# A spectral mixer with a token MLP, forward and backward: x's normal form made again on GpSimd, gradient blocks placed by hand, a mean column moved to TensorE

## The chip, the core and the metric

The kernel runs on one NeuronCore of a Trainium2 chip. A core has five instruction streams that run beside each other and meet only at semaphores: TensorE (PE; its weight loads are listed apart, as PEld), VectorE (DVE), ScalarE (ACT), GpSimd (POOL) and SyncE (SP). SP computes nothing; it issues DMAs, and so does GpSimd here. TensorE multiplies a stationary block of at most 128 x 128 (the weights, "lhsT") by a moving block and adds up in PSUM; ScalarE and VectorE copy results from PSUM to SBUF, the working memory of 128 partitions. GpSimd works on SBUF alone in this kernel.

The metric is the device time of one execution in microseconds, lower is better.

## What is computed

The function has two residual blocks on x of 2048 x 448 (S x D, bfloat16), and the kernel returns its output and its gradients for a given grad_out with respect to x, w_r, w_i, w1, b1, w2 and b2.

```python
def _A_ref(x, w_r, w_i):                     # spectral mixer
    X = rfft2(x.astype(float32))             # over S and D; 225 columns kept
    y = irfft2(X * (w_r + 1j * w_i), s=(S, D)).astype(bfloat16)
    return y

def _B_ref(x, w1, b1, w2, b2):               # MLP over the tokens, F = 1792
    h = layernorm(x)
    u = gelu(einsum("bsd,sf->bdf", h, w1) + b1)
    y = einsum("bdf,fs->bds", u, w2) + b2
    return y.transpose(0, 2, 1)

h  = x + _A_ref(layernorm(x), w_r, w_i)
h2 = h + _B_ref(layernorm(h), w1, b1, w2, b2)
out, vjp = jax.vjp(f, x, w_r, w_i, w1, b1, w2, b2); grads = vjp(grad_out)
```

## The kernel before

All tables of the Fourier transforms are constants in DRAM; the transforms themselves are matmuls. A sequence of 2048 rows is held as 16 row tiles of 128 partitions (`NT = 16`), F as 14 blocks of 128 (`NFB = 14`).

The stages, in the order of TensorE's work:

1. Forward rows. x is loaded in four groups of four row tiles. `Norm` (line 298) takes the statistics on DVE (`bn_stats`), the square root on ACT, and writes xln = x * rstd + nb, where nb = -mean * rstd, partly on ACT and partly on DVE. `nb` is a small buffer from a ring. `fft_rows` (331) folds a group into even and odd parts (`eo`, two vector operations and a copy), multiplies by `kf` (342) and copies the results to `zt`.
2. `dg` (468 and on): grad_out times w2, 14 blocks of 16 matmuls (472), each with a transposed load of w2 (`w2T`, ring of four). These blocks need nothing of stage 1 and fill TensorE between the matmuls of `fft_cols` (346), `ifft_cols` (405) and the forward inverse rows, `ifft_rows` (438).
3. `cmul` (389) is the complex product with the filter, on DVE, over six groups of columns (`R_GROUPS`).
4. `gelu_in`, `gelu_out`, `gelu_back` (554 to 586): hidden layer, its activation g and du, the gradient ahead of it. `gb1`, the sum of du over the tokens, is a by-product; line 606 copies it into column D of `du`, so that the matmuls of stage 6 sum it too, as a mean of a row of dh.
5. Output of the forward pass with w2 (`w2c`, 627).
6. dh (666 to 684): for each of 16 row tiles 14 matmuls of w1 transposed with du (449 columns), then `norm_back` (643), the gradient of the layer norm, with the row's mean from column D. Groups of four finished row tiles are folded and transformed by `fft_rows` as they come.
7. The backward mixer: `fft_cols`, `cmul` with w_b, `ifft_cols` give ab2. Then 16 backward rows, `ifft_rows` and `norm_back` with the normal form of x (`xr`) and rstd_x, give the gradient of x.
8. Weight gradients: 14 blocks `gw2(j)` and 16 blocks `gw1(h)`. A block multiplies transposed copies (`g_t` and `goT`, or `hlnT` and `du_t`) in `outer` (200): twelve matmuls over three full slices of D (206) and four over the last 64 columns (213), which go to the two halves of the array. For that the last 64 columns lie twice, in partitions 0 to 63 and 64 to 127 (`ld_twice`). ACT, or DVE for one quarter in some blocks, copies the four PSUM banks to an `s6` or `s4` buffer (ring `w4`, four buffers), and GpSimd issues the store. `grad_w` (749) is another `cmul`, which gives the gradients of w_r and w_i.

Orders. The program is written once, and a scheduler orders the instructions of each engine; where the source gives no order, it takes ready work by its priority. Before, the source has all 16 backward rows, then all gw2 blocks from 1 on, then the gw1 blocks, and the scheduler mixes gradient matmuls in between the rows. `issue_after` puts an instruction behind another one in its engine's order. `nxt` chains SP's loads of the first half in the order of the source; SP issues them one after the other, and an issue can wait for a buffer. The forward's normal form of x is stored to DRAM by four DMAs of this chain (lines 490-491), and read back four row tiles at a time as `xr` by GpSimd's queue (715-717).

`norm_back`, in short: ACT forms v = rstd * ps (+ nm1 in dh's case) in one of three `f2` buffers; DVE forms the row sum nm2 of v times xhat, then xhat * nm2 + v, then adds the residual gradient.

Of the kernel before, what the change touches and what calls it, by code (L numbers as in the profile page):

```python
# [17 lines left out]
P = 128  # L18
S = 2048
D = 448  # L20
# [97 lines left out]
def kernel(  # L118
# [170 lines left out]

    xln_d = dram.tile([P, NT, D], BF16, name="xln_d")  # L290
    xs_d = dram.tile([P, 2, XW], BF16, name="xs_d")
# [6 lines left out]
    class Norm:  # L298
        def __init__(self, src, dst, rstd, eps_col, scale, nm):
            self.src, self.dst, self.rstd, self.eps_col, self.scale, self.nm = src, dst, rstd, eps_col, scale, nm  # L300

        def stats(self, h):
# [9 lines left out]
        def finish(self, g):  # L312
            mv = self.mv[:, :].rearrange("p (i c) -> p i c", c=2)
            r = self.rstd[:, 4 * g:4 * g + 4]
            sq = col(4, f"sq_{self.nm}")
            ac.activation(out=sq[:], in_=mv[:, :, 1], func=ACT.Sqrt, bias=self.eps_col[:], scale=self.scale)
            ve.reciprocal(out=r, in_=sq[:])
            nb = col(4, f"nb_{self.nm}")
            ve.scalar_tensor_tensor(out=nb[:], in0=mv[:, :, 0], scalar=-1.0, in1=r, op0=ALU.mult, op1=ALU.mult)
            for i in range(4):  # L320
                h = 4 * g + i

                if (i > 1 or g == 3) if self.nm == "x" else (i > 1 and g == 3):
                    ve.tensor_scalar(out=self.dst[:, h, :], in0=self.src[:, h, :], scalar1=self.rstd[:, h:h + 1],
                                     scalar2=nb[:, i:i + 1], op0=ALU.mult, op1=ALU.add)
# [62 lines left out]

    def cmul(out, a, b, conj, done=None):
        for r0, r1 in R_GROUPS:  # L390
            n = (r1 - r0) * DF
# [45 lines left out]

    def ifft_rows(ab, itab, h):
        a_t = itab[:, 0:2 * DF].rearrange("p (c k) -> p c k", c=2)
# [4 lines left out]
        for c in range(2):  # L444
            pe.matmul(pq[:, DF:], lhsT=ab[:, 1, c, h, :, :], rhs=b_t[:, c, :], start=(c == 0), stop=(c == 1))  # L445
        eo = k1([P, 2 * DF], "eo2")
        ev(eo[:], pq[:], "a")
        py = ps_sp([P, D])
        pe.matmul(py[:, 0:DF], lhsT=kinv[:, 0, :], rhs=eo[:, 0:DF], start=True, stop=False)  # L449
# [63 lines left out]
    for h in range(NT):  # L513
        py = ifft_rows(ab, di0, h)
        ve.tensor_tensor(out=hn[:, h, :], in0=py[:], in1=x[:, h, :], op=ALU.add)
# [89 lines left out]
    keep(du_d, du, NFB - 2, NFB)  # L605
    ve.tensor_copy(out=du[:, :, D], in_=gb1[:])

# [35 lines left out]
    def norm_back(ps, mean, xhat, rstd_c, back, base, out):  # L643

        v = f2([P, D], "v")
        if mean:
            nm1 = col(1, "nm1")
            ve.tensor_scalar(out=nm1[:], in0=ps[:, D:D + 1], scalar1=rstd_c, scalar2=-1.0 / D,  # L648
                             op0=ALU.mult, op1=ALU.mult)
            ac.activation(out=v[:], in_=ps[:, 0:D], func=ACT.Identity, scale=rstd_c, bias=nm1[:])  # L650
# [62 lines left out]
    ifft_cols(w_b, ab2)  # L713
    for h in range(NT):
        if h % 4 == 0:
# [3 lines left out]
        gx = k1([P, D], "gx")  # L719
        norm_back(py, False, xr[:, h % 4, :], rstd_x[:, h:h + 1], -1.0 / D, dh[:, h, :], gx[:])  # L720
        st(rows(out_1[0])[:, h, :], gx[:])


# [11 lines left out]

    for j in range(1, NFB):
        gw2(j, "aaaa" if j < 8 else "aaav")


# [6 lines left out]
    xs_b = slot(4, [P, 2, XW], "xs_b")  # L746


    def grad_w():
        ld(xs_b[:], xs_d[:])  # L750
        o2 = out_2.rearrange("(q r) k -> q (r k)", r=NR)
        o3 = out_3.rearrange("(q r) k -> q (r k)", r=NR)

        def out(r0, r1):
            return xs_b[:, 0, r0 * DF:r1 * DF], xs_b[:, 1, r0 * DF:r1 * DF]

        def done(r0, r1, last):
            st(o2[:, r0 * DF:r1 * DF], xs_b[:, 0, r0 * DF:r1 * DF])
            st(o3[:, r0 * DF:r1 * DF], xs_b[:, 1, r0 * DF:r1 * DF])

        cmul(out, ds, xs_b, True, done)

# [60 lines left out]
```

## Time and profile before

| what | us |
|---|---|
| median of 3 runs | 367.74 |
| lowest and highest run | 366.51, 368.8 |
| the profiled execution | 367.85 |
| its span, from first to last instruction | 366.1 |
| PE busy in it | 343.1 |
| DVE, ACT, POOL busy in it | 232.3, 210.7, 58.0 |

How the lines are read. In the page, part 1 has busy time, share and count for each engine; part 2 cuts the span into 40 slices and gives the busy share of each as a digit. A timeline row has its start, its duration, the engine ("SPq" is SP's queue: the time that an issue holds it), the line, the operation, output<-inputs, and in brackets how long the engine was idle before it and who ended that. A group of the table of lines has its count after an x, then busy time and mean nanoseconds of one, then the idle time before its members and what ended it. A row of the table of stretches has the stretch, its length, then the busy time and count of PE, PEld, DVE, ACT and POOL, the granted TensorE clock, the busy share of the DMA engines and GB/s. A DMA row has its count, the size of one, and the microseconds from issue to landing. Matmuls overlap, so that one group's busy time runs into the next; distances between starts are safer.

### The profile page before, as it was taken

The page shows a single profiled execution, that of the slowest core. Times are in us where ns is not written, and L with a number is a line of the kernel's source. Part 1 is how long each engine was busy: PE and PEld are TensorE (multiplying, and loading weights), DVE is VectorE, ACT ScalarE, POOL GpSimd, SP SyncE. Part 2 cuts the span into 40 slices and gives each one's busy share as a digit, 9 for nine tenths or more (in the row PEclk, how much of TensorE's full clock was granted, in tenths as well). Part 3 has the DMA queues.
Part 4 walks back from the last instruction along what each step waited for, and adds up shares of the span by engine and source line. Part 5 has one row for each costly group of instructions (what it writes and reads, how often), then busy time and mean ns, then how long its engine had stood idle before and what let it go on. Part 6 is the DMA issues. An engine that isn't in the chain of part 4 may idle for free. (4 is left out here: it accounts for less than half of the span.)

```text
span 366.1 us, 5758 instructions
## 1 busy us (share of the span) xinstructions
PE 343.1 (94%) x2115; PEld 190.9 (52%) x2115; DVE 232.3 (63%) x550; ACT 210.7 (58%) x415; POOL 58.0 (16%) x105
## 2 busy tenths in 40 slices
PE   0899998999999999999999999899999999999994
PEld 0556665676655555555554556355664455544442
DVE  4882779887746999522157778637995555699200
ACT  3474553447649997005612243787767666767573
POOL 1000000001122112400340000100121232337310
PEclk9999999999999999999999999999999999999999
DMA  8999999999799999999999879592598356848634
GB/s 284 254 228 337 235 291 259 298 236 312 230 320 181 311 327 215 376 329 308 216 262 237 175 147 280 116 233 88 145 218 259 140 192 231 306 166 288 228 139 163
DMA packets 132989, 87.47 MB, mean 239 GB/s; under 512 B 92033, under 2 KB 123905, under 8 KB 132577
## 3 DMA queue, kind: packets, MB, share of 16 engines
q1 hardware_dynamic: 124768, 56.77, 66.8%
q0 software_dynamic: 8048, 30.31, 22.6%
q8 instruction: 16, 0.26, 0.3%
q14 instruction: 13, 0.10, 0.1%
q10 hardware_dynamic: 144, 0.03, 0.0%
HBM read 32.81 MB, written 30.76 MB: 174 GB/s over the span
## 5 line engine op out<-in xcount | busy, mean ns | idle before, releaser
L225 ACT CAST s<-ps_mm 128x512 bf16<-128x512 f32 x98 | 50.8, 571 | 27.7 <-PE ps_mm L213 18.0
L472 PE MATMUL ps_mm<-go_nat,w2T 128*128 128x448 bf16 x224 | 51.2, 362 | 1.4 <-DMA w2T<-in_B_w_dram 1.4
L683 PE MATMUL ps_mm<-du,w1T 128*128 128x449 bf16 x224 | 43.6, 353 | 0.3 <-DMA w1T<-in_B_w_dram 0.3
L206 PE MATMUL ps_mm<-goT,g_t 128*128 128x512 bf16 x168 | 41.8, 379 | 0.0
L176 POOL DMA_DIRECT2D out_dram<-s x29 | 15.6, 539 | 118.3 <-ACT s L225 102.7
L683 PEld LDWEIGHTS <-w1T 128*128 128x128 bf16 x224 | 21.7, 97 | 21.3 <-DMA w1T<-in_B_w_dram 0.8
L650 ACT ACTIVATE v<-ps_mm,nm,rstd_h 128x448 f32<-128x448 f32 x16 | 11.6, 725 | 36.7 <-DVE nm L648 36.7
L627 PEld LDWEIGHTS <-w2c 128*128 128x128 bf16 x224 | 21.9, 98 | 20.5
L559 PEld LDWEIGHTS <-w1c 128*128 128x128 bf16 x224 | 21.8, 98 | 19.9 <-issue 1.0
L472 PEld LDWEIGHTS <-w2T 128*128 128x128 bf16 x224 | 21.9, 100 | 17.6 <-DMA w2T<-in_B_w_dram 2.7
L206 PE MATMUL ps_mm<-du_t,hlnT 128*128 128x512 bf16 (+1 forms) x144 | 30.4, 353 | 0.0
L627 PE MATMUL ps_mm<-gT,w2c 128*128 128x448 bf16 x112 | 30.3, 352 | 0.0
L627 PE MATMUL ps_sp<-gT,w2c 128*128 128x448 bf16 x112 | 30.3, 352 | 0.0
L206 PEld LDWEIGHTS <-hlnT 128*128 128x128 bf16 x192 | 17.9, 98 | 19.8 <-issue 4.6
L381 DVE TENSOR_TENSOR gg<-ps_sp,gi 128x450 bf16<-128x450 f32 x28 | 16.2, 621 | 18.0 <-ACT gi L378 17.9
L559 PE MATMUL ps_mm<-hln,w1c 128*128 128x448 bf16 x112 | 23.8, 352 | 0.3 <-ACT hln L327 0.3
L206 PEld LDWEIGHTS <-g_t 128*128 128x128 bf16 x168 | 16.1, 97 | 14.0 <-issue 1.1
L559 PE MATMUL ps_sp<-hln,w1c 128*128 128x448 bf16 x112 | 22.8, 352 | 0.0
L225 ACT CAST eo<-ps_sp 128x450 bf16<-128x450 f32 x32 | 17.2, 538 | 9.5 <-PE ps_sp L445 9.2
L655 DVE CUSTOM_DVE_ANT_0 junk<-v,xr 128x448 bf16<-128x448 f32 x16 | 10.0, 624 | 19.8 <-ACT v L652 19.8
L639 ACT ACTIVATE junk<-go_r 128x448 bf16<-128x448 bf16 x16 | 9.2, 576 | 22.7 <-DMA go_r<-in_grad_out_dram 22.2
L632 DVE SCALAR_TENSOR_TENSOR h<-ps_mm,b2col,hr 128x448 bf16<-128x448 f32 x8 | 5.1, 679 | 25.8 <-PE ps_mm L627 25.8
(151 smaller groups left out, 653.1 us busy)
## 6 DMA issues: line engine op xcount, KB each, us to landing
w1c<-in_B_w_dram SPq DMA_DIRECT2D x7, 1024.0 KB, 8.7
w2c<-in_B_w_dram SPq DMA_DIRECT2D x8, 896.0 KB, 13.6
out_dram<-s POOLq DMA_DIRECT2D x14, 512.0 KB, 4.1
out_dram<-s POOLq DMA_DIRECT2D x15, 448.0 KB, 2.9
xs_d<-xs SPq DMA_DIRECT2D x1, 1800.0 KB, 7.6
xs_b<-xs_d SPq DMA_DIRECT2D x1, 1800.0 KB, 8.1
x<-in_A_x_dram SPq DMA_DIRECT2D x4, 448.0 KB, 4.4
go_nat<-in_grad_out_dram SPq DMA_DIRECT2D x2, 896.0 KB, 7.1
```

What stands on the lines that cost most here:

```text
L176: return (eng or po).dma_start(out=out, in_=in_)
L206: last = pe.matmul(ps, lhsT=lhs[:, c, a], rhs=rhs[:, c, b], start=opens and c == 0, stop=not opens and c == 2)
L225: return ac.copy(out=out, in_=in_)
L381: last = ve.tensor_tensor(out=gg[:], in0=pr[:], in1=gi[:], op=op)
L472: pe.matmul(pg[:], lhsT=w2T[j][:, t, :], rhs=go_nat[:, t, :], start=(t == 0), stop=(t == NT - 1))
L559: pe.matmul(pu[:], lhsT=wc[:, h, o:o + P], rhs=hln[:, h, :], start=(h == 0), stop=(h == NT - 1))
L627: pe.matmul(p2[i][:], lhsT=w2c[t0 // 4][:, j, i * P:(i + 1) * P], rhs=gT[:, j, :], start=(j == 0), stop=(j == NFB - 1))
L632: ve.scalar_tensor_tensor(out=h2[:], in0=p2[i][:], scalar=b2col[:, t:t + 1], in1=hr[:, i, :], op0=ALU.add, op1=ALU.add)
L639: ac.activation(out=junk[:], in_=go_r[:, h, :], func=ACT.Copy, accum_out=gb2[:, h:h + 1])
L650: ac.activation(out=v[:], in_=ps[:, 0:D], func=ACT.Identity, scale=rstd_c, bias=nm1[:])
L655: ve.tensor_tensor_reduce(out=junk[:], in0=v[:], in1=xhat, scale=back, scalar=0.0, op0=ALU.mult, op1=ALU.add, accum_out=nm2[:])
L683: w1_last = pe.matmul(pd[:], lhsT=w1T[:, j, :], rhs=du[:, j, 0:D + 1], start=(j == 0), stop=(j == NFB - 1))
```

## The change

Four things change.

- xln isn't stored to DRAM. `Norm` keeps all its nb in a constant tile. For the backward rows x itself is loaded into `xr` (a ring of its own, two buffers), and GpSimd forms x * rstd_x + nb in place, one operation for each row tile.
- The order of the backward rows is written out. `ifft_rows` is split into `rows_mid` (first half, with its copy to SBUF) and `rows_out` (second half). The first halves run two rows ahead. Behind each row stands one gradient block: gw2(6) to gw2(13) behind rows 0 to 7, gw1(0) to gw1(7) behind rows 8 to 15; gw2(1) to gw2(5) come before the rows. `grad_w` is cut into its six groups, one behind each of rows 10 to 15. In gw2(6) to (13) DVE copies the last of four banks, and ACT all of them in gw2(1) to (5); before, DVE had that share from gw2(8) on.
- dh's mean: column D of du gets gb1 * (-1/D) instead of gb1, so that `nm1` is the PSUM column times rstd. That product is now made by ACT, where DVE made it with the factor.
- Loads. The transposed load of g_t and the second copies of g_t's and goT's last 64 columns are put ahead of the loads of w_b. The first two w1c loads come with dg blocks 7 and 10 instead of 5 and 9.

```diff
-    xln_d = dram.tile([P, NT, D], BF16, name="xln_d")
...
+            self.nb = consts.tile([P, NT], F32, name=f"nb_{nm}")
...
-            nb = col(4, f"nb_{self.nm}")
-            ve.scalar_tensor_tensor(out=nb[:], in0=mv[:, :, 0], scalar=-1.0, in1=r, op0=ALU.mult, op1=ALU.mult)
+            nb = self.nb[:, 4 * g:4 * g + 4]
+            ve.scalar_tensor_tensor(out=nb, in0=mv[:, :, 0], scalar=-1.0, in1=r, op0=ALU.mult, op1=ALU.mult)
...
-    def cmul(out, a, b, conj, done=None):
-        for r0, r1 in R_GROUPS:
+    def cmul(out, a, b, conj, done=None, groups=R_GROUPS):
+        for r0, r1 in groups:
...
-    for g in range(4):
-        nxt(ld, xln_d[:, 4 * g:4 * g + 4, :], xln[:, 4 * g:4 * g + 4, :])
...
-        if j in (5, 9, 13):
+        if j in (7, 10, 13):
             load_w1c(nxt)
...
-    ve.tensor_copy(out=du[:, :, D], in_=gb1[:])
+    ve.tensor_scalar(out=du[:, :, D], in0=gb1[:], scalar1=-1.0 / D, scalar2=None, op0=ALU.mult)
...
-            ve.tensor_scalar(out=nm1[:], in0=ps[:, D:D + 1], scalar1=rstd_c, scalar2=-1.0 / D,
-                             op0=ALU.mult, op1=ALU.mult)
+            ac.activation(out=nm1[:], in_=ps[:, D:D + 1], func=ACT.Copy, scale=rstd_c)
...
+    g_t = slot(0, [P, 4, F], "g_t")
+    ld_t4(g_t[:], gT_d[:])
+    ld_twice(g_t, w1T_last)
+    ld_twice(goT, w1T_last)
     with tc.issue_after(w1T_last.ins):
         load_w(w_b, lambda load, out, in_: load(out, in_))
     fft_rows(dh, zt2, 2, "aava")
-    g_t = slot(0, [P, 4, F], "g_t")
-    ld_t4(g_t[:], gT_d[:])
-    ld_twice(goT, w1T_last)
-    ld_twice(g_t, w1T_last)
...
+    for j in range(1, 6):
+        gw2(j, "aaaa")
+    mids = [rows_mid(ab2, di1, h) for h in range(2)]
     for h in range(NT):
+        if h + 2 < NT:
+            mids.append(rows_mid(ab2, di1, h + 2))
         if h % 4 == 0:
-            xr = e4([P, 4, D], "xr")
-            ld(xr[:], xln_d[:, h:h + 4, :], po)
-        py = ifft_rows(ab2, di1, h)
+            xr = ring.tile([P, 4, D], BF16, tag="xr", bufs=2, name="xr")
+            ld(xr[:], rows(A_x[0])[:, h:h + 4, :], po)
+            for i in range(h, h + 4):
+                po.tensor_scalar(out=xr[:, i - h, :], in0=xr[:, i - h, :], scalar1=rstd_x[:, i:i + 1],
+                                 scalar2=nx.nb[:, i:i + 1], op0=ALU.mult, op1=ALU.add)
+        with tc.issue_after(mids[-1][1].ins):
+            py = rows_out(mids[h][0])
         gx = k1([P, D], "gx")
         norm_back(py, False, xr[:, h % 4, :], rstd_x[:, h:h + 1], -1.0 / D, dh[:, h, :], gx[:])
         st(rows(out_1[0])[:, h, :], gx[:])
+        if h < 8:
+            gw2(h + 6, "aaav")
+        else:
+            gw1_four(h - 8)
+        if h == 7:
+            ld(xs_b[:], xs_d[:])
+        if h > 9:
+            grad_w(R_GROUPS[h - 10])
...
-    for j in range(1, NFB):
-        gw2(j, "aaaa" if j < 8 else "aaav")
...
-    for h in range(8):
+    def gw1_four(h):
         outs, out = gw1(h, ps_mm)
         outer(outs[:2], outs[2:], hlnT, du_t)
         out()
-        if h == 3:
-            grad_w()
```

More of the change, by code (lines that the diff above doesn't have):

```diff
@@ L444, in ifft_rows, with rows_out @@
         for c in range(2):
-            pe.matmul(pq[:, DF:], lhsT=ab[:, 1, c, h, :, :], rhs=b_t[:, c, :], start=(c == 0), stop=(c == 1))
+            last = pe.matmul(pq[:, DF:], lhsT=ab[:, 1, c, h, :, :], rhs=b_t[:, c, :], start=(c == 0), stop=(c == 1))
         eo = k1([P, 2 * DF], "eo2")
         ev(eo[:], pq[:], "a")
+        return eo, last
+    def rows_out(eo):
         py = ps_sp([P, D])
@@ L713 @@
     ifft_cols(w_b, ab2)
-    for h in range(NT):
-        if h % 4 == 0:
-            xr = e4([P, 4, D], "xr")
-            ld(xr[:], xln_d[:, h:h + 4, :], po)
-        py = ifft_rows(ab2, di1, h)
-        gx = k1([P, D], "gx")
-        norm_back(py, False, xr[:, h % 4, :], rstd_x[:, h:h + 1], -1.0 / D, dh[:, h, :], gx[:])
-        st(rows(out_1[0])[:, h, :], gx[:])
     def small_out(dst, src, n):
@@ L746 @@
     xs_b = slot(4, [P, 2, XW], "xs_b")
[L749 to L761, printed above, removed]
     def gw1(h, ps):
```

18 lines of the change are left out of this document (16 added, 2 removed).

## The prediction

> **What bounds the kernel now.** I read the page first: parts 1 and 2 for the engine that is full, then the chain, then stretches of the timeline around the edits.
>
> ```profile
> span 366.1 us, 5758 instructions
> PE 343.1 (94%) x2115; PEld 190.9 (52%) x2115; DVE 232.3 (63%) x550; ACT 210.7 (58%) x415; POOL 58.0 (16%) x105
> PE   0899998999999999999999999899999999999994
> ```
>
> PE is busy 343.1 of 366.1 us, and no slice but the edges is under 8 tenths. The built program of the changed kernel has the same 4232 TensorE rows, in the same order up to the first backward row tiles. So no TensorE work goes: the change is worth the waits of PE that it removes, less those that it adds. The profiled run took 367.85 us, 1.75 over its span and 0.1 above the median of 367.74; I sum against 367.85. One per cent, about what a measurement of this kernel can tell from no change, is 3.7 us.
>
> **Start: two loads come first.** The instruction order shows what the source doesn't. The first two loads of x for the backward rows, and their eight GpSimd operations, stand at the front of GpSimd's queue, right behind the two bias loads.
>
> ```profile
> 1.92 0.54 POOL L173 DMA_DIRECT2D b2r<-in_B_b_dram  x1
> 3.06 7.43 SPq L179 DMA_TRANSPOSE w2T<-in_B_w_dram  x1
> 10.54 1.05 SPq L173 DMA_DIRECT2D x<-in_A_x_dram  x2
> 12.62 0.13 PEld L472 LDWEIGHTS <-w2T 128*128 128x128 bf16 x2 [0.25 <-DMA w2T<-in_B_w_dram]
> 37.45 1.06 PEld L472 LDWEIGHTS <-w2T 128*128 128x128 bf16 x7 [0.25 <-DMA w2T<-in_B_w_dram]
> 3.00:9.00 6.00, 0.00 (x0) 0.00 (x0) 3.90 (x13) 1.31 (x3) 0.00 (x0) 1.00 1.06 385
> 12.00:18.00 6.00, 6.00 (x34) 3.07 (x33) 4.66 (x16) 3.33 (x7) 0.00 (x0) 1.00 1.02 252
> xr<-xln_d POOLq DMA_DIRECT2D x4, 448.0 KB, 9.3
> w1c<-in_B_w_dram SPq DMA_DIRECT2D x7, 1024.0 KB, 8.7
> ```
>
> The last bias load is issued at 2.46 us, so both loads go out by 3.6 us, into the stretch from 3 to 9 us in which the DMA engines are full (share 1.06, the second number from the end) at 385 GB/s. SP's queue is backed up there: one transpose holds it for 7.43 us, and the last two loads of x stand behind that. PE's first dg matmul ends its wait on a w2T transpose at 12.62 us, and at 37.45 it waits for one again: until then PE runs at the pace of SP's loads. Two loads of 448 KB are 0.918 MB. At 385 GB/s they take 2.4 us, at the 252 GB/s of 12 to 18 us 3.6, and nothing if they fit into holes. I take 2.4: they are plain loads like those of the first stretch. All that stands behind them, w2T and the last groups of x, lands that much later, and PE with it: **+2.4 us** (0 to 3.6).
>
> The GpSimd operations have no row; its only computing rows are memsets of one column. DVE's form of the operation bounds one from below, its two-input form doubled from above; GpSimd must neither beat DVE nor be trusted to match it.
>
> ```profile
> L324 DVE TENSOR_SCALAR xln<-x,rstd_x,nb_x 128x448 bf16<-128x448 bf16 x10 | 3.4, 392 | 0.1
> L657 DVE SCALAR_TENSOR_TENSOR junk<-hln,nm,v 128x448 bf16<-128x448 bf16 x16 | 11.0, 685 | 0.6
> ```
>
> So 0.39 to 1.37 us; I take 0.7, the plain two-input row, and nothing for it in the sum: xr is read in the last quarter of the run, and what stands behind them on GpSimd's queue, the stores of hn, comes only with the first forward rows. The Trainium skill, GPSIMD Engine Reference, section 3.1, gives 1.03 to 1.8 cycles an element at 1.2 GHz; that is an estimate of 0.39 to 0.67 us, with the sum unchanged.
>
> **xln isn't stored.** Four stores of 448 KB leave SP's queue, where they stood ahead of two w2T transposes.
>
> ```profile
> 43.00 2.79 SPq L173 DMA_DIRECT2D xln_d<-xln  x4
> 47.70 8.16 SPq L179 DMA_TRANSPOSE w2T<-in_B_w_dram  x2
> 56.50 0.55 PE L472 MATMUL ps_mm<-go_nat,w2T 128*128 128x448 bf16 x2 [1.12 <-DMA w2T<-in_B_w_dram]
> 58.04 0.63 DVE L396 TENSOR_TENSOR t_r<-xs,w_t 128x900 bf16<-128x900 bf16 x1 [0.49 <-ACT xs L356]
> 60.00:70.00 10.00, 10.00 (x73) 6.92 (x72) 9.81 (x18) 4.44 (x9) 0.00 (x0) 1.00 1.28 274
> 76.35 0.30 PEld L472 LDWEIGHTS <-w2T 128*128 128x128 bf16 x3 [0.62 <-DMA w2T<-in_B_w_dram]
> ```
>
> 1.84 MB at 385 GB/s are 4.8 us of the queue, more than the 1.12 that PE waits at 56.5. But DVE is the next to be late: it is busy 9.81 of the 10 us from 60 on, and had idled only 0.49 before 58.04. Of the wait only that 0.5 is gained. The wait at 76.35 goes as well, since the transposes up to there no longer queue behind xln or the first w1c loads (moved from block 5 to 7); PE's weight load idled 0.62 for it, of which I take 0.4, as a matmul runs into it. The store of xs moves ahead of one transpose and SP's issue of the first w1c pair slips behind both; I cost that at nothing, as gelu's matmuls read it only behind all fourteen dg blocks (if that cover is gone, PE waits for part of a landing, 8.7 us in all). **-0.9 us** (-0.5 to -1.6).
>
> **dh: ScalarE forms the mean column, and g_t's copy goes before w_b.** -1/D now sits in du's last column, so the vector operation on one column becomes one of ScalarE, ahead of v.
>
> ```profile
> L648 DVE TENSOR_SCALAR nm<-ps_mm,rstd_h 128x1 f32<-128x1 f32 x16 | 3.4, 211 | 0.0
> L650 ACT ACTIVATE v<-ps_mm,nm,rstd_h 128x448 f32<-128x448 f32 x16 | 11.6, 725 | 36.7 <-DVE nm L648 36.7
> L655 DVE CUSTOM_DVE_ANT_0 junk<-v,hln 128x448 bf16<-128x448 f32 x16 | 10.0, 626 | 9.8 <-ACT v L650 9.8
> 222.52 5.53 PE L683 MATMUL ps_mm<-du,w1T 128*128 128x449 bf16 x28
> 227.23 0.21 DVE L648 TENSOR_SCALAR nm<-ps_mm,rstd_h 128x1 f32<-128x1 f32 x1
> 229.99 0.21 DVE L648 TENSOR_SCALAR nm<-ps_mm,rstd_h 128x1 f32<-128x1 f32 x1
> 230.59 0.85 PE L213 MATMUL ps_mm<-goT,g_t 64*128 64x512 bf16 x4 [0.36 <-DMA g_t<-g_t]
> 232.45 0.39 DVE L658 TENSOR_TENSOR go_r<-junk,go_r 128x448 bf16<-128x448 bf16 x1
> 234.19 1.07 PE L342 MATMUL ps_sp<-kf,eo 128*128 128x128 bf16 x16 [1.34 <-DVE eo L336]
> L316 ACT ACTIVATE sq_h<-mv_h,eps_h 128x4 f32<-128x4 f32 x4 | 1.2, 298 | 4.0 <-DVE mv_h L308 4.0
> ```
>
> Rows 14 and 15 end on PE at about 225.2 and 228.0, yet DVE takes their column at 227.23 and 229.99, as it works off the rows before. With ScalarE (nearest row: 0.30 us for four columns) v of row 15 is there at 228.0 + 0.2 for the handover + 0.3 + 0.7 = 229.2. DVE then needs 0.63 + 0.69 + 0.39 and a short read, 1.8 us a row without idling, and some 0.2 for a copy in its way: row 15 ends at 231.2 instead of 232.84 (232.45 + 0.39). The fold after it takes the same 1.35 us to PE, so 234.19 becomes 232.6. PE is ready by 234.19 - 1.34 - 0.36 = 232.5, as g_t's copy no longer stands behind w_b's two loads. I take **-1.6 us** (0 to -2.2). Elsewhere in dh PE never waits for this chain, so nothing comes of it there.
>
> **Backward rows: a gw2 or gw1 block fixed behind each, rows two ahead.** Before, the inverse row's second half waits for its copy eo, which stands in ScalarE's order between the copies of a gradient block.
>
> ```profile
> 309.33 0.27 PE L449 MATMUL ps_sp<-eo,kinv 128*128 128x225 bf16 x1
> 327.18 0.26 PE L449 MATMUL ps_sp<-eo,kinv 128*128 128x225 bf16 x1 [0.30 <-ACT eo L225]
> 327.96 1.46 PE L206 MATMUL ps_mm<-du_t,hlnT 128*128 128x512 bf16 x6
> 331.34 0.26 PE L449 MATMUL ps_sp<-eo,kinv 128*128 128x225 bf16 x1 [0.30 <-ACT eo L225]
> 335.50 0.26 PE L449 MATMUL ps_sp<-eo,kinv 128*128 128x225 bf16 x1 [0.30 <-ACT eo L225]
> 341.16 0.60 PE L213 MATMUL ps_mm<-du_t,hlnT 64*128 64x512 bf16 x4
> 346.77 0.60 PE L213 MATMUL ps_mm<-du_t,hlnT 64*128 64x512 bf16 x4
> L225 ACT CAST s<-ps_mm 128x512 bf16<-128x512 f32 x98 | 50.8, 571 | 27.7 <-PE ps_mm L213 18.0
> L225 ACT CAST eo<-ps_sp 128x450 bf16<-128x450 f32 x32 | 17.2, 538 | 9.5 <-PE ps_sp L445 9.2
> L396 DVE TENSOR_TENSOR t_r<-ds,xs_b 128x1350 bf16<-128x1350 bf16 (+1 forms) x6 | 4.7, 782 | 0.8 <-DMA xs_b<-xs_d 0.7
> ```
>
> Where nothing interrupts, two gw1 blocks take 346.77 - 341.16 = 5.61 us, 2.8 each. A row's own matmuls take 327.96 - 327.18 = 0.78. A row with a block is thus 3.6 us of PE, but the last rows come every 4.16. From 309.33 to 335.50 PE does seven rows and six and a half blocks, 5.5 + 18.2 = 23.7 us, in 26.2: 2.5 us of waits. In the new order eo is copied two rows before it is read. ScalarE then has four gradient copies, eo and v: 3.5 x 0.57 (the fourth is half as wide) + 0.54 + at most the 0.73 of dh's v = 3.3 of 3.6 us. That still fits, by little. I take **-2.4 us** (-3.2 with the gw2 rows' small waits, +0.8 if ScalarE's order binds by 0.4 a row over eight). DVE has 1.8 us a row and, in the last six, a sixth of grad_w: two products of 4.7 us and two sums over half the elements, some 15 us, so 4.3 against 3.6. It falls 4 us behind, which three buffers of v, 10 us of rows, take up.
>
> On GpSimd's queue the third and fourth xr loads wait for a row on DVE, and four operations wait for the landing (9.3 us); the stores of s and gx behind them are late by about 10 us, where four buffers of s give 4 x 3.6 = 14.
>
> **The sum.** 367.85 + 2.4 - 0.9 - 1.6 - 2.4 = 365.35, so **365.4 us**. The scaling of du's last column takes the place of a copy of it, under the forward output's matmuls, and costs nothing; the row products in grad_w are the same work in other places.
>
> **Rivals.**
> A, the early loads are free: they fit beside SP's transposes, which at 12 to 18 us move only 252 GB/s. Against it stands the share of 1.02 there, engines full with small packets. 365.4 - 2.4 = 363.0.
> B, the row waits move instead of going: fixed blocks make PE wait for ScalarE's copies each row, or DVE's lag reaches v. ScalarE at 3.3 of 3.6 us speaks for it, the two rows' lead against. 365.4 + 2.4 = 367.8.
> C, slower: the eight early GpSimd operations hold up DVE. They fall between 8 and 25 us, when DVE makes the folds that PE's first matmuls wait for. If a GpSimd operation shuts DVE out and takes the upper 1.37 us, that is 11 us in 17, of which DVE, busy 4.66 of 6, has 3.8 free; of the other 7.2, PE waits 2.4 for its loads anyway: 365.4 + 4.8 = 370.2. It decides from 0.8 us an operation, where eight fill 3.8 + 2.4. The Trainium skill, SBUF — State Buffer, section Who interferes with whom, states this as an exclusive lock: a GpSimd instruction that reads SBUF and a DVE one with two SBUF inputs, or in a two-port mode, block each other for a whole instruction. The trace of before has no GpSimd operation that could show it.
> D, nothing arrives: the waits return a few us later at DVE or ScalarE, and only the early loads count: 367.85 + 2.4 = 370.3.
>
> **Chances.** Forecast 0.45, A 0.18, B 0.20, C 0.10, D 0.07. Faster than 364.1 needs A or the forecast's better end, where the start costs under 1 us: 0.15 + 0.15 = 0.30. Slower than 371.4 are the far ends of C and D, with the early loads at their 3.6 us: 0.07. Within 1%: 0.63. The range holds the forecast, A down to 1 us below it and B up to 1.5 above it, and leaves out C, D and the far end of A: 362.0 to 369.3.
>
> **What would show it.** The first dg matmul at about 15 us instead of 12.6, and dg's waits on w2T at 56 and 76 gone; GpSimd rows near 0.7 us; PE's L342 group ahead of the backward columns with under 0.8 us of wait; the backward rows 3.6 us apart with gw1 and 3.9 with gw2. DVE rows in the first 25 us much longer than 0.39 and 0.63 would speak for C, an unmoved 12.6 for A, and row distances above 4 for B.

## The result, and the profile after

| what | before | after |
|---|---|---|
| median of 6 runs, us | 367.88 | 363.64 |
| lowest and highest run, us | 366.51, 368.8 | 363.04, 364.02 |
| ratio, with its 95% interval | | 0.9901 (0.9881 to 0.9921) |
| span of the profiled execution, us | 366.1 | 362.1 |

The kernel is 4.2 us faster; by the interval of the ratio, 2.9 to 4.4. The forecast was 365.4, a gain of 2.5. (Medians here and below are over all runs; ratios leave out the runs of a kernel that lie more than 1.5% above its fastest.) Part 1 of the page of the changed kernel, and PE's row of slices:

```profile
span 362.1 us, 5793 instructions
PE 339.8 (94%) x2100; PEld 191.2 (53%) x2115; DVE 233.5 (64%) x536; ACT 213.8 (59%) x429; POOL 71.7 (20%) x121
PE   0599999999999999999999999999999999999995
```

PE is as full as before (94%), and it is later into its work: the second slice is 5, where it was 8. The timeline of the changed kernel shows why. The first row is GpSimd's issue of the two early loads of x; then come its operations on them, and PE's weight loads that wait for w2T.

```profile
2.45 1.12 POOL L173 DMA_DIRECT2D xr<-in_A_x_dram  x2
9.46 3.71 POOL L786 TENSOR_SCALAR xr<-xr,rstd_x,nb_x 128x448 bf16<-128x448 bf16 x4 [5.88 <-DMA xr<-in_A_x_dram]
14.90 0.13 PEld L475 LDWEIGHTS <-w2T 128*128 128x128 bf16 x2 [1.40 <-DMA w2T<-in_B_w_dram]
40.67 1.06 PEld L475 LDWEIGHTS <-w2T 128*128 128x128 bf16 x7 [1.05 <-DMA w2T<-in_B_w_dram]
57.11 1.86 PE L475 MATMUL ps_mm<-go_nat,w2T 128*128 128x448 bf16 x9
76.26 0.92 PE L475 MATMUL ps_mm<-go_nat,w2T 128*128 128x448 bf16 x4
```

The first dg block starts 2.3 us late (14.91 against 12.62) and the sixth 3.2 (40.67 against 37.45). Block 8 begins within the nine matmuls from 57.11 on, and block 11 comes behind the four from 76.26; neither row has a bracket, so both waits on w2T are gone.

The same timeline further on: the last dh rows, the fold of the last group (L342), then the second halves of the last backward rows.

```profile
231.95 0.39 DVE L659 TENSOR_TENSOR go_r<-junk,go_r 128x448 bf16<-128x448 bf16 x1
233.69 1.07 PE L342 MATMUL ps_sp<-kf,eo 128*128 128x128 bf16 x16 [0.31 <-DVE eo L336]
314.10 0.26 PE L452 MATMUL ps_sp<-eo,kinv 128*128 128x225 bf16 x1
317.80 0.26 PE L452 MATMUL ps_sp<-eo,kinv 128*128 128x225 bf16 x1
328.48 0.26 PE L452 MATMUL ps_sp<-eo,kinv 128*128 128x225 bf16 x1
331.78 0.26 PE L452 MATMUL ps_sp<-eo,kinv 128*128 128x225 bf16 x1
```

The fold waits 0.31 us where it waited 1.34. The rows no longer wait for eo: with the first halves of the rows ahead those with gw1 come every 3.7 us, where the last ones came every 4.16, and every 3.3 when none is left to run ahead. (Those with gw2 are 4.02 apart, from 302.70 to 306.72, as from 297.28 to 301.30 before: they had no wait to give.) Two groups of the table of lines of the changed kernel, with the last number before the bar the mean of one in ns:

```profile
L650 ACT ACTIVATE nm<-ps_mm,rstd_h 128x1 f32<-128x1 f32 x16 | 4.2, 261 | 37.0 <-PE ps_mm L684 37.0
L786 POOL TENSOR_SCALAR xr<-xr,rstd_x,nb_x 128x448 bf16<-128x448 bf16 x16 | 13.6, 856 | 12.1 <-DMA xr<-in_A_x_dram 9.9 <-DVE nb_x L319 2.1
```

To see where the time went, the program is cut at instructions that every version has. The stages are distances between starts of PE rows: the first dg matmul; the first of the sixth block; the first of the fourteenth; the first dh matmul; the first of the last dh row; the fold of the last group; the first and the last second half of a backward row; the end. Starts before: 12.62, 37.45, 87.57, 182.68, 225.21, 234.19, 278.20, 335.50, 366.08. Starts after: 14.91, 40.67, 89.25, 184.37, 226.41, 233.69, 277.81, 331.78, 362.14.

| stage, us | before | after | difference |
|---|---|---|---|
| to the first dg matmul | 12.62 | 14.91 | +2.29 |
| dg blocks 0 to 5 | 24.83 | 25.76 | +0.93 |
| dg blocks 5 to 13 | 50.12 | 48.58 | -1.54 |
| block 13 to the first dh row | 95.11 | 95.12 | 0 |
| dh, first to last row | 42.53 | 42.04 | -0.49 |
| last dh row to the fold | 8.98 | 7.28 | -1.70 |
| fold to the first backward row | 44.01 | 44.12 | +0.11 |
| backward rows | 57.30 | 53.97 | -3.33 |
| to the end | 30.58 | 30.36 | -0.22 |

The differences add up to the 3.9 us between the two ends. The change costs at the start and gains in the stages behind it. Which part of it does each was tried out.

One cut is not quite fair. In the new order the first halves of two more rows, 8 matmuls of about 0.1 us each, stand ahead of the first backward row: PE's weight loads number 295 and 343 in the two stages around it before, and 302 and 336 after. So the row stage has some 0.8 us less to do, and the stage ahead of it that much more. The two together went from 101.31 to 98.09 us: 3.2 is the gain to reckon with.

### The profile page after: what moved, and what is told of

The parts are those of the page before. It is cut to its first block, busy times and chain, and to the rows that moved or that the text cites. A ratio compares the mean times of both kernels' runs of the same rounds, so it can differ in the third digit from the quotient of the medians.

```text
span 362.1 us, 5793 instructions
## 1 busy us (share of the span) xinstructions
PE 339.8 (94%) x2100; PEld 191.2 (53%) x2115; DVE 233.5 (64%) x536; ACT 213.8 (59%) x429; POOL 71.7 (20%) x121
## 4 chain that ended last, share of the span: by engine, by line
PE 79%; DMA 7%; DVE 6%; ACT 5%; issue 1%; SPq 1%; ACTq 0%
PE ps_mm L206 15%; PE ps_mm L684 12%; PE ps_mm L475 8%; DMA w2T<-in_B_w_dram 7%; PE ps_mm L560 6%; PE ps_mm L629 6%; PE ps_sp L629 6%; PE ps_sp L560 5%; PE ps_mm L213 3%; PE ps_sp L413 2%; PE ps_sp L206 2%; PE ps_sp L414 2%; PE ps_sp L443 2%; PE ps_sp L445 2%; PE ps_sp L353 1%; ACT s L225 1%
## 5 line engine op out<-in xcount | busy, mean ns | idle before, releaser
L225 ACT CAST s<-ps_mm 128x512 bf16<-128x512 f32 x96 | 48.1, 566 | 24.9 <-PE ps_mm L213 17.8
L206 PE MATMUL ps_mm<-goT,g_t 128*128 128x512 bf16 x158 | 40.7, 379 | 0.4 <-issue 0.2
L650 ACT ACTIVATE nm<-ps_mm,rstd_h 128x1 f32<-128x1 f32 x16 | 4.2, 261 | 37.0 <-PE ps_mm L684 37.0
L206 PEld LDWEIGHTS <-g_t 128*128 128x128 bf16 x168 | 15.6, 98 | 15.0 <-issue 3.4
L342 PE MATMUL ps_sp<-kf,eo 128*128 128x128 bf16 x128 | 9.3, 231 | 12.7 <-DVE eo L336 12.2
L225 ACT CAST zt<-ps_sp 128x512 bf16<-128x512 f32 x26 | 13.5, 596 | 8.3 <-PE ps_sp L342 8.2
```

Source lines behind the costliest of these rows:

```text
L206: last = pe.matmul(ps, lhsT=lhs[:, c, a], rhs=rhs[:, c, b], start=opens and c == 0, stop=not opens and c == 2)
L225: return ac.copy(out=out, in_=in_)
L342: last = pe.matmul(pz[:, c, :], lhsT=eo[:, i, o:o + P], rhs=kf[:], start=True, stop=True)
```

## The experiments

Each kernel is the changed one with one edit, if nothing else is said. They ran in three groups on different chips; the kernel before had medians of 367.0 (29 runs), 366.77 (17) and 366.42 (23) beside them. Ratios are to these, and stages are cut as above.

**The early loads moved behind the forward output.**

```diff
+            with tc.issue_after(h2_last.ins) if h < 8 else nullcontext():
-            ld(xr[:], rows(A_x[0])[:, h:h + 4, :], po)
+                ld(xr[:], rows(A_x[0])[:, h:h + 4, :], po)
```

> The first two loads of x for the backward rows, with their eight GpSimd operations, stand behind the last store of the forward output instead of at the front of GpSimd's queue. Theory 1 (the loads cost at the start what they take of the DMA engines): the first dg matmul is back at 12.6 us from 14.9, and the sixth block at 37.4 from 40.7; of these 2.3 to 3.2 us as much stays in the time as DVE and the later w2T loads don't take back. By the prediction's term the time is 363.6 - 2.4 = 361.2; if what was given back further on (1.9 at the ninth block, 1.7 at the first w1 matmul) comes again as waits, 361.9. Rival A (the early loads are free): 363.6.

Measured: 365.38 us, 360.39 to 376.6 in 12 runs, ratio 0.9898 (0.9857 to 0.994). The first dg matmul is at 12.55 and the sixth block at 37.25, so the start is back to that of before, and at the first dh row the kernel is 3.4 us ahead of the changed one (180.94 against 184.37). Then it loses more than that. PE's timeline of this kernel, SP's queue in it, and the table of stretches (the granted clock is third from the end):

```profile
195.08 7.21 PE L684 MATMUL ps_mm<-du,w1T 128*128 128x449 bf16 x28 [3.25 <-DMA w1T<-in_B_w_dram]
183.81 16.62 SPq L179 DMA_TRANSPOSE w1T<-in_B_w_dram  x4
195.00:200.00 5.00, 4.92 (x17) 2.15 (x18) 2.35 (x4) 0.32 (x2) 3.48 (x4) 0.66 1.07 138
```

The two loads are now issued at 183.86, in the same instant as the transposed load of w1T that PE needs next. It lands 11.2 us after its issue (183.81 to 195.04); in the changed kernel, with no loads beside it, the first of these took 5.7 (187.39 to 193.05). Four transposes hold SP's queue for 16.6 us here (all twelve for 37.0, against 32.5 in the changed kernel). PE waits 3.25 us, and its clock is granted at 0.66 for the 5 us after. dh takes 47.13 us instead of 42.04. So the first theory holds at the start, and the place that I chose for the loads was as bad as the old one.

The same kernel once more on another chip:

> The kernel with late loads again, a second profile on another chip of runs: every row distance within 0.1 us of its first profile, the time within 0.5 us of it.

Measured: 364.7 us in one run; the first dg matmul at 12.28, dh in 45.45 us with a wait of 3.07 for w1T. It misses the expectation, as dg blocks 0 to 5 took 25.80 us and not 24.70, and dh differs by 1.7: what waits for transposes varies from run to run by a microsecond or more.

**GpSimd's operations alone, at the start.** As the kernel with late loads, and in the loop over the four groups of the forward:

```diff
     folded.append(fft_rows(xln, zt, g, "avav" if g == 3 else "aaaa"))
+    for i in range(4 * g, 4 * g + 4):
+        xg = ring.tile([P, D], BF16, tag="xg", bufs=2, name="xg")
+        po.tensor_scalar(out=xg[:], in0=x[:, i, :], scalar1=rstd_x[:, i:i + 1],
+                         scalar2=nx.nb[:, i:i + 1], op0=ALU.mult, op1=ALU.add)
```

> Like the run with late loads, but with sixteen more GpSimd operations of the same form at the start, four as each group's rstd is there, which read x in SBUF and write a scratch tile that nobody reads. They load nothing. Theory 1 (loads are the cost): as the run with late loads, within 0.3 us. Rival C (GpSimd's operations hold up DVE): slower than it by up to 16 x 0.7 = 11 us if each shuts DVE out for its length and DVE is what is late; by 1 to 3 us if only the folds ahead of PE's first matmuls are hit; DVE rows in the first 30 us grow by 0.4 us and more.

Measured: 369.94 us (362.81 to 371.98), ratio 0.9953 (0.9917 to 0.9988), against 0.9898 with late loads alone: 2 us more, with intervals that overlap. In the profiled execution (370.88) most of the excess is the wait for w1T in dh again, 5.87 us here, which says nothing of the operations; only what lies ahead of 90 us is read. The fourteenth dg block starts at 87.53, against 85.83 and 86.66 in the two profiles without these operations: 0.9 to 1.7 us for sixteen. In the table of lines of this kernel, with DVE's row from the first 60 us:

```profile
L469 POOL TENSOR_SCALAR xg<-x,rstd_x,nb_x 128x448 bf16<-128x448 bf16 x16 | 15.2, 962 | 10.7 <-DVE nb_x L319 5.3 <-issue 5.2 <-POOL xg L469 0.2
L324 DVE TENSOR_SCALAR xln<-x,rstd_x,nb_x 128x448 bf16<-128x448 bf16 x10 | 5.0, 545 | 0.1
```

Both sides stretch: DVE's rows to 545 ns from 391 in the kernel with late loads, and GpSimd's to 962 in the mean: nine of its sixteen operations take 0.71 to 0.73 us, four take 1.53. Rival C's mechanism exists, but at the start it comes to a tenth of a microsecond an operation, not to the length of one.

**Loads early, operations late.** This separates the two in the changed kernel itself: the operations of the first two xr stand behind the store of gw2(0).

```diff
+            with tc.issue_after(gw2_first.ins) if h < 8 else nullcontext():
-            for i in range(h, h + 4):
-                po.tensor_scalar(...)
+                for i in range(h, h + 4):
+                    po.tensor_scalar(...)
```

> The changed kernel with the two loads still at the start, but their eight GpSimd operations behind gw2(0)'s store. If the loads alone make the late start: first dg matmul 14.4 to 14.9 and sixth block 40 to 40.7 as in the changed kernel, and 363.6. If the operations have a share (DVE held up): the sixth block up to 0.8 us earlier, and 362.8.

Measured: 364.0 us (363.33 to 365.39), ratio 0.9938 (0.9916 to 0.9959). First dg matmul 14.46, sixth block 40.08, as in the other kernels with early loads. So the loads make the late start, and the operations beside them nothing that shows. The fold-to-rows stage takes 44.75 us instead of 44.12: the operations now lie beside the backward columns, where PE waits 0.57 us for a gg sum of DVE.

**Loads and operations behind gw2(0).**

```diff
-    gw2(0, "aaaa")
+    gw2_first = gw2(0, "aaaa")
...
+            with tc.issue_after(gw2_first.ins) if h < 8 else nullcontext():
-            ld(xr[:], rows(A_x[0])[:, h:h + 4, :], po)
+                ld(xr[:], rows(A_x[0])[:, h:h + 4, :], po)
```

> The changed kernel with the first two loads of x for the backward rows, and their eight GpSimd operations, behind the store of gw2(0) at about 235 us, where no transpose that PE waits for is on its way. By the rows of the runs so far: the start returns to that of before (first dg matmul 12.3 to 12.8, sixth block 37.2 to 38.1), and the w1T rows of dh stay 2.7 us apart, so 363.6 less 2.4 to 3.4 = 360.2 to 361.2. If the eight operations between 240 and 248 us hold up DVE there: up to 1.5 us more, 361.7 to 362.7. If the start's delay is taken up further on: 363.6.

Measured: 362.43 us (361.17 to 365.79), ratio 0.9889 (0.984 to 0.9937). The start is back (12.25, 37.45), dh is undisturbed (42.04), and at the fold the kernel is 3.2 us ahead of the changed one (230.46 against 233.69). At the first backward row 1.1 is left (276.71 against 277.81). The timeline of this kernel, one row each of GpSimd, DVE and PE:

```profile
252.25 4.80 POOL L787 TENSOR_SCALAR xr<-xr,rstd_x,nb_x 128x448 bf16<-128x448 bf16 x5
252.79 2.98 DVE L396 TENSOR_TENSOR t_r<-ds,w_b 128x1350 bf16<-128x1350 bf16 x1 [0.67 <-ACT ds L356]
256.47 1.15 DVE L381 TENSOR_TENSOR gg<-ps_sp,gi 128x450 bf16<-128x450 f32 x2
257.14 0.35 PE L353 MATMUL ps_sp<-gg,hf 128*128 128x450 bf16 x1 [1.95 <-DVE gg L381]
```

And the same DVE row in the changed kernel, where GpSimd does nothing at that time:

```profile
256.02 0.86 DVE L396 TENSOR_TENSOR t_r<-ds,w_b 128x1350 bf16<-128x1350 bf16 x1 [0.67 <-ACT ds L356]
```

One product of cmul takes 2.98 us instead of 0.86. The 2.1 us more are the length of three GpSimd operations of 0.7, which run from 252.96 to 255.06; the next one, beside DVE's next products, takes 2.00. The gg sum that PE needs stands behind it in DVE's order, and PE waits 1.95. This is rival C's mechanism at more than its full length, three operations running, in a place that the prediction did not look at.

**xln stored again.**

```diff
+    xln_d = dram.tile([P, NT, D], BF16, name="xln_d")
...
+    for g in range(4):
+        nxt(ld, xln_d[:, 4 * g:4 * g + 4, :], xln[:, 4 * g:4 * g + 4, :])
...
-            ld(xr[:], rows(A_x[0])[:, h:h + 4, :], po)
-            for i in range(h, h + 4):
-                po.tensor_scalar(...)
+            ld(xr[:], xln_d[:, h:h + 4, :], po)
```

> The changed kernel with xln stored to DRAM by four DMAs of SP's chain again, and xr read back from it; GpSimd has no operation, and no load of xr can come before the stores. All else as changed. Set against the run with late loads it is the price of the stores alone. Prediction's term: 0.9 us over it (361.2 + 0.9 = 362.1). By the trace of after, where the wait at 56 us went in full: 1.3 + 0.4 = 1.7 over it (362.9). If DVE is what is late there in any case: equal to it.

Measured: 366.26 us (363.56 to 367.82), ratio 0.9972 (0.9944 to 1.0); the profiled execution, with a span of 361.5, lies at the low end of these. The start is that of before (12.75, 37.20), and dg blocks 5 to 13 take 51.15 us against 48.58 without the stores. PE's timeline of this kernel, and the read-backs on GpSimd's queue:

```profile
57.72 0.55 PE L476 MATMUL ps_mm<-go_nat,w2T 128*128 128x448 bf16 x2 [2.54 <-DMA w2T<-in_B_w_dram]
49.82 0.57 POOL L173 DMA_DIRECT2D xr<-xln_d  x1 [47.35 <-DMA xln_d<-xln]
```

The wait on w2T is back, and longer than the 1.12 of before; the first two read-backs now go out right behind the stores and cross the transposes too, which is the likely reason. The expected 1.7 us for the stores thus can't be read from this run cleanly; the next but one has the stores without the early read-backs. The row stage takes 53.97 us with GpSimd idle in it, exactly as with its operations: beside the new order of the rows they cost PE nothing.

**w1c loads back at blocks 5 and 9.**

```diff
-        if j in (7, 10, 13):
+        if j in (5, 9, 13):
```

> The changed kernel with the first two w1c loads at dg blocks 5 and 9 again, instead of 7 and 10. If the move is what ended the wait on w2T at 76 us, PE waits there again by up to 0.44 us, and the time is 364.0; if leaving xln out did that, 363.6, and SP issues the w1c loads earlier with nothing gained from it.

Measured: 362.95 us (362.45 to 364.79), ratio 0.9906 (0.9871 to 0.9941). Blocks 5 to 13 take 48.58 us, to the hundredth as in the changed kernel. The place of these loads does nothing here; leaving xln out ended both waits. (The next kernel, with the stores, has both again, 0.57 us at 55.86 and 0.53 at 75.97.)

**The order of the backward rows, alone.** The kernel before with the new rows; xln is stored, w1c, the mean column and the copies are as before, and the first two read-backs come behind the store of gw2(0).

> The kernel before with the new order of the backward rows alone: xln is stored at the start and read back as xr (the first two read-backs behind gw2(0)'s store, the ring of xr its own), w1c, the mean column and the copies of g_t as before; only nb stays in a constant tile. If the order is what gives the last stage its gain without the rest: from the fold of the last row group to the end 128.4 us instead of 131.9, and 367.9 - 3.5 = 364.4. By the prediction's term 367.9 - 2.4 = 365.5. If the gain needs GpSimd to make xr: 367.9.

Measured: 363.07 us (362.29 to 363.6), ratio 0.9898 (0.9859 to 0.9936). This one part gives as much as the whole change (0.9901). The rows in PE's timeline of this kernel:

```profile
316.96 0.26 PE L453 MATMUL ps_sp<-eo,kinv 128*128 128x225 bf16 x1
320.65 0.26 PE L453 MATMUL ps_sp<-eo,kinv 128*128 128x225 bf16 x1
```

They are 3.69 us apart, and the stage takes 53.97 us, 3.33 less than before; with the 44.39 of the stage ahead of it, 2.95 less. The pieces of the order (rows ahead, fixed blocks, grad_w in six, DVE's share of the copies, xr's own ring) were not tried one by one. Blocks 5 to 13 take 49.81 us: the stores cost 1.2 us there, between this kernel and the changed one.

**The order of the rows undone.** All sixteen rows in the source first, halves together, then gw2, gw1 and grad_w in one piece; xr is still made by GpSimd.

```diff
-    mids = [rows_mid(ab2, di1, h) for h in range(2)]
     for h in range(NT):
-        if h + 2 < NT:
-            mids.append(rows_mid(ab2, di1, h + 2))
...
-        with tc.issue_after(mids[-1][1].ins):
-            py = rows_out(mids[h][0])
+        py = rows_out(rows_mid(ab2, di1, h)[0])
...
-        if h < 8:
-            gw2(h + 6, "aaav")
-        else:
-            gw1_four(h - 8)
...
+    for j in range(1, NFB):
+        gw2(j, "aaaa" if j < 8 else "aaav")
...
+    for h in range(8):
+        gw1_four(h)
```

> The changed kernel with the order of before from the backward rows on: all sixteen rows in the source first, the halves of a row together, then gw2(1) to gw2(13), then gw1, grad_w in one piece behind gw1(3), DVE's quarter from gw2(8) on. xr and all else as changed. The prediction's term: 363.6 + 2.4 = 366.0. By the distance between the two traces from 274 us on: 363.6 + 3.2 = 366.8, with waits of 0.3 us on eo in the rows again. Rival B or D (the waits only move): 363.6.

Measured: 368.09 us (366.7 to 370.77), ratio 1.0045 (1.002 to 1.0071): slower than before. The row stage takes 60.91 us, 3.6 more than in the kernel before with this order; but the profiled execution took 370.06 us, 2.0 above the median, so that a usual run should have about 1.6 of them (an estimate). The timeline of this kernel, in order of cause, and two stretches with their clock:

```profile
316.93 6.82 POOL L721 TENSOR_SCALAR xr<-xr,rstd_x,nb_x 128x448 bf16<-128x448 bf16 x4 [7.23 <-DMA xr<-in_A_x_dram]
324.29 1.07 POOL L176 DMA_DIRECT2D out_dram<-s  x2
327.18 1.84 ACT L225 CAST s<-ps_mm 128x512 bf16<-128x512 f32 x4 [2.91 <-DMA out_dram<-s]
327.82 1.24 PE L206 MATMUL ps_mm<-du_t,hlnT 128*128 128x512 bf16 x5 [2.04 <-ACT s L225]
```

```profile
324.00:328.00 4.00, 1.80 (x11) 0.81 (x12) 4.00 (x9) 1.09 (x3) 4.00 (x8) 1.00 0.72 268
328.00:332.00 4.00, 3.55 (x18) 1.66 (x16) 4.00 (x9) 2.10 (x5) 2.39 (x6) 0.70 0.94 318
```

GpSimd's queue stands 7.23 us for the last xr to land, and then four operations take 1.7 us each, as grad_w's products run on DVE beside them. No store leaves the queue from 309.70 to 323.70, 14 us. That uses up the four s buffers, ScalarE waits 2.91 us for one, and PE 2.04 for ScalarE. With the clock at 0.70 behind that, the wait costs once more. In the new order the buffers carry such a delay: in the kernel with w1c back and in the one with the loads behind gw2(0) the same load takes 8.5 and 8.9 us to land, as the 8.8 here (308.02 to 316.83), and the row stage takes 53.97 us all the same.

**dh: the mean column on DVE again.**

```diff
-    ve.tensor_scalar(out=du[:, :, D], in0=gb1[:], scalar1=-1.0 / D, scalar2=None, op0=ALU.mult)
+    ve.tensor_copy(out=du[:, :, D], in_=gb1[:])
...
-            ac.activation(out=nm1[:], in_=ps[:, D:D + 1], func=ACT.Copy, scale=rstd_c)
+            ve.tensor_scalar(out=nm1[:], in0=ps[:, D:D + 1], scalar1=rstd_c, scalar2=-1.0 / D,
+                             op0=ALU.mult, op1=ALU.mult)
```

> The changed kernel with dh's mean column as before: du's column D is gb1, and DVE makes nm1 with the factor -1/D. The copies of g_t and goT stay ahead of w_b. The prediction puts nearly all of its 1.6 us on this part, since DVE's chain behind the last row tile is what PE waits for: 363.6 + 1.3 = 364.9 or a little more. If the order of the loads gave it instead: 363.6.

Measured: 364.37 us (363.62 to 364.55), ratio 0.9929 (0.9909 to 0.9949). From the last dh row to the fold 8.26 us against 7.28: the mean column is worth 0.98.

**dh: the copies of g_t and goT behind w_b again.**

```diff
-    g_t = slot(0, [P, 4, F], "g_t")
-    ld_t4(g_t[:], gT_d[:])
-    ld_twice(g_t, w1T_last)
-    ld_twice(goT, w1T_last)
     with tc.issue_after(w1T_last.ins):
         load_w(w_b, lambda load, out, in_: load(out, in_))
     fft_rows(dh, zt2, 2, "aava")
+    g_t = slot(0, [P, 4, F], "g_t")
+    ld_t4(g_t[:], gT_d[:])
+    ld_twice(goT, w1T_last)
+    ld_twice(g_t, w1T_last)
```

> The changed kernel with the copies of the last 64 columns of g_t and goT behind the loads of w_b again; the mean column stays with TensorE and ScalarE. gw2(0)'s four last matmuls wait for the copy by 0.4 to 0.5 us again, so 364.1 if PE then goes on at once; 363.6 if the wait for the fold hides it; 365.2 if this order is worth the whole 1.6 us.

Measured: 363.34 us (362.85 to 363.8), ratio 0.9903 (0.9881 to 0.9925); 7.27 us to the fold. The copy of g_t lands at 229.79, ahead of the matmuls that read it at 230.99. The order of these loads gives nothing.

**Both undone.**

> The changed kernel with both parts of dh undone: nm1 on DVE with the factor there, and the copies of g_t and goT behind w_b. In the two traces 1.7 us lie between the first matmul of the last dh row and the fold behind it (8.98 against 7.28); the mean column alone undone gave 8.26, the copies alone 7.27. If the two need each other: 8.98 again, and 363.6 + 1.7 = 365.3. If the copies never count: 8.26, and 364.4 as with the mean column alone.

Measured: 364.52 us (363.83 to 365.56), ratio 0.995 (0.993 to 0.997). The fold in PE's timeline of the kernel with the mean column undone, with the copies undone, and with both:

```profile
234.15 1.07 PE L342 MATMUL ps_sp<-kf,eo 128*128 128x128 bf16 x16 [1.30 <-DVE eo L336]
```

```profile
233.30 1.07 PE L342 MATMUL ps_sp<-kf,eo 128*128 128x128 bf16 x16 [0.30 <-DVE eo L336]
```

```profile
234.11 1.07 PE L342 MATMUL ps_sp<-kf,eo 128*128 128x128 bf16 x16 [1.25 <-DVE eo L336]
```

8.22 us with both undone, as with the column alone. The 8.98 of the kernel before does not come back, so 0.7 us of it come from that execution and not from the parts undone here. The kernel with only the new rows, whose dh is that of before, has 8.25 too, and 42.04 for dh. The trace of before tells what these had that they did not, in SP's, GpSimd's and DVE's rows around the last forward outputs (h):

```profile
156.57 6.66 SPq L173 DMA_DIRECT2D go_r<-in_grad_out_dram  x2
180.12 0.54 POOL L176 DMA_DIRECT2D out_dram<-gb2b  x1 [25.54 <-ACT gb2b L641]
185.57 1.28 DVE L632 SCALAR_TENSOR_TENSOR h<-ps_sp,b2col,hr 128x448 bf16<-128x448 f32 x2 [1.98 <-PE ps_mm L683]
```

In that one execution go_r was issued at 156.57, where the other profiles have 144 to 156, and the store of gb2b, which waits for sums over go_r, went out only 2.6 us ahead of the first dh row, where the others have 6.0 to 12.5. The stores of h stand behind it on GpSimd's queue, and DVE does its last two h rows at 185.57, in the second row of dh (185.37); in the kernel with both parts undone it does them at 184.67, ahead of that. (The row names PE as the releaser, but in that kernel the same rows run before the matmul named; a buffer of h, freed by a store, is what is left.) So DVE makes its first nm of dh 4.08 us behind PE's first dh matmul (186.76), against 2.89 in that kernel (186.73). From the first nm to the last it then takes 43.2 us in both, and PE's rows take 42.0 where they do not wait, so such a delay of 1.2 us isn't made up. Of it 0.49 are covered, as PE itself lost them in dh at a late w1T (one row took 3.16 us instead of 2.68), and 0.7 are left behind the last row. With the column on ScalarE the nm rows keep step with PE, 42.0 us, and there the column's gain comes from. That chain is read from the trace; why the loads came late in that execution was not tried.

## Why the prediction was near, and where its terms were off

Direction and range held, and of each of the four terms the main mechanism. Two side parts did nothing: the later place of w1c and the earlier copy of g_t. That the sum came this near is in part luck: start and dh came out worse than forecast, by 0.3 and 0.6 us, which hid most of what rows and xln gave beyond their terms.

**Start, +2.4.** Right, and a little small. Seven kernels with early loads have the first dg matmul at 14.45 to 14.91 (mean 14.57), seven without at 12.25 to 12.75 (mean 12.46): 2.1 us. At the sixth block it is 40.16 against 37.47 in the mean, without the kernel that has the extra operations: 2.7. Rival A (the loads are free) is out. What the step missed was that the second wait on w2T, at 40.67, would grow too, from 0.25 to 1.05.

**xln not stored, -0.9.** Mis-sized: 1.2 to 1.5 us. The step took 0.5 of the wait of 1.12, because DVE, full from 60 on, would be late next. It was not: in blocks 5 to 13 PE takes 48.58 to 48.59 us in nine profiles without the stores, whatever their start, and 48.69 and 48.76 in the two others. The likely reason is that a full engine is late only for work that needs it, and of what the dg blocks read only w2T was on its way. The later place of w1c, to which part of the wait at 76 was put down, does nothing.

**dh, -1.6.** The column gives 0.98, where the step has nearly all of 1.6. DVE's last row did end 0.5 us earlier than before (231.95 against 232.45), though the row itself began 1.2 later. The new chain was worked out rightly: the fold comes 7.28 us behind the first matmul of the last row, where the step has 232.6 - 225.21 = 7.39. What it had wrong is what to set it against, 8.98 where 8.2 is usual. That PE would be ready by then because of g_t's earlier copy was no part of it: undone, it costs nothing. The trace's 1.70 agreed with the forecast only because the profiled execution of before carried 0.7 us that belongs to neither part.

**Backward rows, -2.4.** The mechanism held, and the size was near the better end of the range: 2.95 us alone and 3.2 in the whole change. The step took the 2.5 us of waits that it counted from 309 us on, and would have had 3.2 with small waits of the gw2 rows; those rows are mostly 4.02 us apart before and after, with one wait of 0.35 at 281.65, so the rest came from elsewhere. Five waits for eo have a bracket in the trace of before, 1.4 us together, and a row with 0.30 in its bracket comes 0.47 later than one without; the remainder is not split up here. ScalarE fits with room: 11.0 us busy in the four rows from 306.72 to 321.49, 2.75 a row where the step had 3.3. Shown twice: alone this order gives 0.9898, and without it the changed kernel is slower than the one before. Rivals B and D are out.

**Rival C** was given 0.10 for the start and fails there. The 0.7 us taken for a GpSimd operation was right (0.712 in the median of the changed kernel); the estimate of 0.39 to 0.67 beside it, whose lower end works out to 0.38, lies just under that. But DVE and GpSimd do hold each other up in these runs, and that decides where GpSimd's operations may stand. The Trainium skill, SBUF — State Buffer, Who interferes with whom, says that a DVE instruction with two SBUF inputs and a GpSimd one that reads SBUF block each other for a whole instruction, and that a DVE instruction with at most one SBUF input outside the two-port modes does not contend. The trace agrees on both: 2.98 against 0.86 us for a product of two SBUF tiles beside GpSimd (here through three instructions and not one), and 1.15 us for two gg sums out of PSUM (1.16 where GpSimd is idle), of which the first runs while GpSimd's last operation does.

**The sum by what was measured:** +2.7 - 1.5 - 1.0 - 3.2 - 0.2 = -3.2, inside the 2.9 to 4.4 of the measurement. The last 0.2 are the end, behind the last row; the two kernels that store xln again have them there as well (30.59 against 30.36 us), so they go with xln, and why was not tried. The rest, to the 4.2 between the medians, is of the size of what the profiled execution of before lost by its late loads (0.49 in dh and 0.7 behind it), and which share of that a usual execution of before has stays open. Taken apart, the change is one part that gains some 3 us, and three that nearly cancel.

No version beats the changed kernel by more than the measurement tells. The loads and operations behind gw2(0) have 0.9889, the rows alone 0.9898, the change 0.9901. Loads behind gw2(0) with the operations behind the backward columns, which would keep the 3.2 us of the start without the 2.1 lost beside GpSimd, was not tried.

## What to carry to other kernels

Before new work is put on an idle engine, look up in the order of its queue where its loads will go out: here two loads whose buffers were free came to stand at the front, and 0.9 MB ahead of the first weights cost 2 to 3 us. A load whose result isn't urgent wants a place where no transposed load that TensorE needs is on its way, and GpSimd's operations a place where DVE does not combine two SBUF tiles on the critical path. Weigh the parts of a change one by one: here one of four carried the gain, and a profile of a single execution of the old kernel gave another part credit for 0.7 us that were the run's.

## What the hardware showed beyond that

- A GpSimd tensor_scalar with two per-row scalars over 128x448 bf16 took 0.705 us at least and 0.712 in the median of 16 in the changed kernel, but 1.7 us in the mean of the four beside grad_w's products with the rows undone.
- Plain loads slow transposed ones that are issued with them: 11.2 us from issue to landing instead of 5.7 for w1T in the kernel with late loads. With the loads behind gw2(0) xr itself lands 15.6 us after its issue when hlnT's transposes run (232.97 to 248.59).
- After a wait TensorE's clock can be granted lower, and not after each: 0.66 over 5 us behind a wait of 3.25 us, 0.70 over 4 us in the run with the rows undone, behind a stretch with PE busy 1.80 of 4 us, but 1.00 behind a wait of 3.07 us in the other profile of the late loads. The Trainium skill, TensorE: Matmul & The Clock Gate, Part 1, has a gate that closes after an idle window of about 3.4 us, and the window runs freely. The last case agrees; in the run with the rows undone no pause of PE was longer than 2.04 us there, so less than a whole idle window was enough.
